# A fused attention, gMLP and expert-attention kernel: a planner with a charge for DVE and POOL in SBUF together, more operations that two engines may take, and new urgency tables

## Chip, cores and metric

The kernel runs on one core of one Trainium2 chip. The metric is the device time of one execution in microseconds (us), as the median of several runs. A core has a matrix engine (PE), three engines that work on tiles in the on-chip memory SBUF and in the matrix engine's result memory PSUM (DVE, ACT, and POOL, which only reads and writes SBUF), and a queue engine (SP) that issues all DMA transfers of this kernel.

## What is computed

Three stages follow each other for 4 batches of 576 tokens and 512 features.

```python
# 1. attention, 8 heads of 64, a window of 64 tokens
scores = q @ k.T / 8;  masked to 0 <= i - j < 64
x = softmax(scores) @ v                        # heads side by side: (4, 576, 512)
# 2. gMLP
h = relu(x @ w_in);  u, v = h[..., :512], h[..., 512:]
v_n = (v - mean(v)) / sqrt(var(v) + 1e-6)
gated = u * (w_spatial @ v_n + b_spatial)
y = gated @ w_out
# 3. four causal attention experts of width 64, the two with the largest gate logits per token
for e in range(4):
    out += gate[e] * (softmax(causal(y @ wq[e] @ (y @ wk[e]).T / 8)) @ (y @ wv[e]) @ wo[e])
```

## The kernel before

**Tiles and precision.** Every product of two full-size operands is made of three matrix passes: each operand is split in a high part and the remainder (`copy` to the high part, `sub` for the rest), and `mm3` adds high times high, high times low and low times high. So each weight and each activation costs a copy and a subtraction on ACT, DVE or POOL before PE can use it. `w_in` and `w_out` come as 64-bit floats: `prep64` loads 512 columns (512 KB), and rebuilds 32-bit values from the two words in four steps, two small ones (the scaled upper word, which only ACT makes, and the sign, which POOL or DVE makes) and two on DVE (`scalar_tensor_tensor`, profile lines L633 and L636), and then copies and subtracts. There are eight such pieces of `w_in` (four for the half V of the hidden layer, four for the half U) and four of `w_out`. `prep_sp` splits the spatial weights.

**Units.** `a_couple` does stage 1 for two groups of 192 queries: 12 score products (tile `sc`), a masked maximum on DVE (L501), the exponential on ACT (L507), two small DVE steps (L520, L522), the division of three 128 x 128 blocks `pa` (POOL or DVE, L512), their transposition on PE (L516), a copy, and 12 products with the values (tiles `pt` and `vt`, `woh`, `wol`). `b_v` projects 128 tokens onto V and normalizes them, `b_u` makes U for 288 tokens and 128 features (12 products), and `b_mix` does the spatial product (14 products of `wsp` and `vh`, `vl`) and the gate. Stage 3 is made in a second phase by `c_qk`, `c_v`, `unit`, `c_pv` and `c_wo`; `fold` first multiplies `w_out` into the weights of stage 3.

**What sets the order.** The program is not issued in the order in which it is written. Each operation is a `Node` with a dictionary of engines that may run it and their assumed costs, its dependencies and its ring buffers. `weave` walks the units and gives each node an urgency, which is the work ahead of it plus a shift from the tables `SHIFT` (one for PE nodes, one for the other engines, one for loads; 351 entries each, by unit). `Planner.run` then goes through assumed time: whenever an engine is free it takes the most urgent node that is ready and has room, unless another engine could end it sooner (`DVE_BIAS`, `POOL_BIAS`, `EFT`). The result is one fixed instruction sequence per engine. On the chip every engine runs its own sequence in order and waits where data is not there. The planner adds `DRAIN` where PE changes between three forms of products (`form` 0 for full-height ones, 1 for the scores of stage 1, 2 for products with the values), and `SWITCH` is the urgency that a change must be worth.

**Heaters.** `heat` issues 68 products of the identity with itself (8 at the start, 60 in slots in which the planner has nothing for PE). Their result is used by nobody.

Loads go over one SP queue in the planned order. A piece of `w_in` stands in one of six `y` tiles (or a `w2` tile), which its predecessor must have left.

Of the kernel before, what the change touches and what calls it, by code (L numbers as in the profile page):

```python
# [58 lines left out]


class Slot:
    def __init__(self, ring):
        self.nth, ring.asked = ring.asked, ring.asked + 1
        self.ring, self.make, self.left, self.free_at, self.t = ring, ring.make, 0, None, None

    def __getitem__(self, key):
        return self.t[key]


class Node:  # L70
    __slots__ = ("on", "emit", "prio", "wait", "next", "ready", "alloc", "use", "end", "by", "late", "form", "nth")


class Planner:
# [2 lines left out]
    ISSUE, WAY, RATE, FLIGHT = 475.0, 650.0, 360.0, 8  # L80
# [1284 lines left out]
```

## Time and profile before

| what | value |
|---|---|
| time, median of 3 runs (lowest, highest) | 463.44 us (463.25, 463.47) |
| profiled execution: time, span of its instructions | 462.36 us, 460.6 us |
| PE busy, share of the span, matrix instructions | 444.6 us, 97%, 3962 |
| DVE busy | 296.2 us, 64% |
| ACT busy | 289.1 us, 63% |
| POOL busy | 159.7 us, 35% |
| mean granted clock of PE | 0.999 of 2.4 GHz |

The span runs from the first to the last instruction of the profiled execution; its time has some 1.8 us around the span. A busy share is the union of an engine's instructions over the span. Matrix instructions overlap each other, so that a busy PE may still stand still between two results; how long PE needs for a block of products is read from the distance of the starts.

### The profile page before, as it was taken

How to read it: one execution, taken by the hardware profiler on the slowest of the kernel's cores; microseconds unless marked ns; L12 is line 12 of the kernel's file. 1: busy time of each engine (PE TensorE's matmuls, PEld its weight loads, DVE VectorE, ACT ScalarE, POOL GpSimd, SP SyncE). 2: the span in 40 equal slices, each digit the busy share in tenths (PEclk: the TensorE clock that was granted, in tenths of full speed). 3: DMA queues.
4: the chain of work that ended last, by engine and by line, in shares of the span. 5: the costliest groups of instructions: out<-in, count | busy, mean ns of one | idle time of the engine just before them, and what ended most of it. 6: DMA issues, size and time to landing. Idle time of an engine off the chain costs nothing.

```text
span 460.6 us, 10987 instructions
## 1 busy us (share of the span) xinstructions
PE 444.6 (97%) x3962; PEld 396.5 (86%) x3962; DVE 296.2 (64%) x1227; ACT 289.1 (63%) x906; POOL 159.7 (35%) x246
## 2 busy tenths in 40 slices
PE   7988998999999999999999999999999999999996
PEld 6766878997799988999899999888988988998875
DVE  3999899556583459912205346987876778858930
ACT  3867894647583337612224436898887797877953
POOL 6689587333831037700541442231031111200100
PEclk9999999999999999999999999999999999999999
DMA  8995334224242131301101000000001001000124
GB/s 268 356 308 161 124 93 156 71 78 135 65 133 61 47 91 52 89 1 54 39 1 21 26 1 2 0 2 1 1 25 46 24 2 22 25 2 1 55 85 137
DMA packets 31624, 32.97 MB, mean 72 GB/s; under 512 B 1937, under 2 KB 25489, under 8 KB 31570
## 3 DMA queue, kind: packets, MB, share of 16 engines
q1 hardware_dynamic: 31570, 32.28, 22.4%
q8 instruction: 31, 0.51, 0.4%
q14 instruction: 23, 0.19, 0.1%
HBM read 27.55 MB, written 4.72 MB: 70 GB/s over the span
## 4 chain that ended last, share of the span: by engine, by line
PE 79%; DVE 7%; DMA 4%; ACT 4%; POOL 3%; issue 1%; SPq 1%; POOLq 0%; ACTq 0%
PE mm L295 56%; PE sc L295 8%; PE at L295 8%; PE at L1180 4%; DMA y<-in_w_in_dram 3%; PE at L516 3%; ACT kd L306 1%; DVE pa L512 1%; POOL pa L512 1%; ACT p L1160 1%; SPq L384 1%; DVE wsp_l L319 1%; DVE xl L319 1%; ACT pg L306 1%; DMA qa<-in_qT_dram 1%
## 5 line engine op out<-in xcount | busy, mean ns | idle before, releaser
L295 PE MATMUL mm<-xh,w 128*128 128x288 f32 x512 | 110.3, 299 | 0.0
L295 PEld LDWEIGHTS mm<-xh,w 128*128 128x128 f32 x512 | 84.3, 188 | 1.2 <-issue 0.9
L295 PE MATMUL mm<-xl,w 128*128 128x288 f32 x256 | 75.4, 294 | 0.0
L295 PE MATMUL mm<-w,xh 128*128 128x512 f32 (+1 forms) x256 | 64.7, 342 | 0.0
L507 ACT ACTIVATE pa<-pa,mx 128x128 f32<-128x128 f32 x144 | 56.0, 395 | 9.7 <-DVE mx L501 9.5
L512 POOL TENSOR_SCALAR pa<-pa,mx 128x128 f32<-128x128 f32 x78 | 34.4, 456 | 54.5 <-ACT pa L507 29.6
L1164 POOL TENSOR_SCALAR p<-p,mc,fx 128x256 f32<-128x256 f32 (+4 forms) x24 | 16.0, 667 | 102.9 <-DVE mc L1163 48.4
L295 PEld LDWEIGHTS mm<-xl,w 128*128 128x128 f32 x256 | 48.2, 188 | 0.2
L295 PEld LDWEIGHTS mm<-w,xh 128*128 128x128 f32 x256 | 43.3, 189 | 5.0 <-issue 0.2
L1160 ACT ACTIVATE p<-p,mc 128x128 f32<-128x128 f32 (+4 forms) x72 | 41.9, 583 | 8.7 <-DVE mc L1148 4.4
L295 PE MATMUL mm<-w,xl 128*128 128x512 f32 (+1 forms) x128 | 43.2, 338 | 0.0
L295 PE MATMUL mm<-wsp_h,vh 128*128 128x288 f32 x128 | 39.0, 305 | 1.6 <-ACT ut L314 1.6
L295 PE MATMUL mm<-wsp_h,vl 128*128 128x288 f32 x128 | 37.7, 295 | 0.0
L295 PE MATMUL mm<-wsp_l,vh 128*128 128x288 f32 x128 | 37.7, 294 | 0.0
L1148 DVE CUSTOM_DVE_ANT_0 p<-sc,cmask 128x128 f32<-128x128 f32 (+4 forms) x72 | 33.7, 482 | 4.8 <-PE sc L295 3.1
L306 ACT ACTIVATE pg<-at 128x512 f32<-128x512 f32 (+4 forms) x80 | 32.3, 432 | 3.9 <-PE at L1180 3.2
L295 PE MATMUL sc<-kd,qs 128*64 128x288 f32 (+5 forms) x96 | 31.5, 342 | 0.1
L1180 PE MATMUL at<-ident,p 128*128 128x128 f32 x192 | 30.3, 276 | 1.0 <-DVE p L1164 0.3
L775 DVE TENSOR_TENSOR y<-mm,ut 128x288 f32<-128x288 f32 x24 | 10.8, 455 | 30.5 <-PE mm L295 30.5
L706 DVE BATCH_NORM_STATS2 st<-vr 128x6 f32<-128x512 f32 (+1 forms) x20 | 13.8, 690 | 25.8 <-ACT vr L314 25.4
L306 ACT ACTIVATE pt<-at 128x384 f32<-128x384 f32 x47 | 21.2, 490 | 14.0 <-PE at L516 14.0
L516 PE MATMUL at<-ident,pa 128*128 128x128 f32 x144 | 24.5, 285 | 5.7 <-DVE pa L512 3.3
(192 smaller groups left out, 1116.2 us busy)
## 6 DMA issues: line engine op xcount, KB each, us to landing
vt<-in_v_dram SPq DMA_DIRECT2D x12, 512.0 KB, 4.2
qa<-in_qT_dram SPq DMA_DIRECT2D x44, 96.0 KB, 3.2
out_dram<-ot SPq DMA_DIRECT2D x15, 256.0 KB, 2.0
y<-in_w_in_dram SPq DMA_DIRECT2D x7, 512.0 KB, 7.0
kt<-in_kT_dram SPq DMA_DIRECT2D x12, 288.0 KB, 3.1
y<-in_w_outT_dram SPq DMA_DIRECT2D x4, 512.0 KB, 3.4
y<-in_wspT_dram SPq DMA_DIRECT2D x2, 576.0 KB, 4.9
ut<-in_kT_dram SPq DMA_DIRECT2D x2, 384.0 KB, 7.5
```

The costliest lines, as they stand in the source:

```text
L295: pe.matmul(o, lhsT, rhs, start=start, stop=stop)
L306: act.activation(o, i, AF.Copy)
L319: engs[e].tensor_tensor(out=o, in0=a, in1=hi.bitcast(F32), op=ALU.subtract)
L507: act.activation(pa[:, j, :], pa[:, j, :], AF.Exp, bias=mx[:, j, 0:1], scale=-1.0, accum_out=mx[:, j, 1:2])
L512: engs[e].tensor_scalar(pa[:, j, :], pa[:, j, :], mx[:, j, 2:3], 1.0, op0=ALU.mult, op1=ALU.mult)
L516: pe.transpose(ps2[:, j * 128:(j + 1) * 128], pa[:, j, :], ident)
L706: a = N((DVE, 600), lambda e: dve.bn_stats(st[:m, 0:6], vr[:m]), [a], alloc=[st], use=[vr])
L775: dve.tensor_tensor(out=o, in0=ps[:, :HS], in1=u[:, d, tk], op=ALU.mult)
L1148: dve.tensor_tensor_reduce(out=P[:, a0:a1], in0=ps[:, :w], in1=msk, scale=-0.125, scalar=3.0e38, op0=ALU.add, op1=ALU.min, accum_out=mc[:, ...
L1160: a = N((ACT, 284 + 0.87 * L), lambda e: act.activation(P[:m, :L], P[:m, :L], AF.Exp, bias=mc[:m, 0:1], scale=-1.0, accum_out=mc[:m, 2:3]) ...
L1164: a = N({POOL: 328 + 0.832 * L, DVE: 90 + 0.52 * L}, lambda e: engs[e].tensor_scalar(P[:, :L], P[:, :L], mc[:, 3:4], fx[:, I, ev:ev + 1], ...
L1180: pe.transpose(ps[:, j * m:(j + 1) * m], P[:, j * 128:(j + 1) * 128], ident)
```

## The change

The planner gets three new rules: the 351 x 3 urgency shifts and the scalar constants are new, some nodes get other assumed costs, and some may go to more engines. What is computed is the same.

- A node that has all its operands in SBUF is marked `sbuf=True`. If such a node starts on DVE while POOL is busy (or on POOL while the last node on DVE was of that kind), the planner lengthens it by 0.55 of the overlap (`CLASH`).
- A load that is issued while earlier ones are still on their way is assumed to land 2.2 us later (`BEHIND`).
- `DRAIN` no longer charges a change into form 0, but takes 78 ns off where a form 1 or 2 node follows one of its kind, and the costs of some PE nodes move by -74 to +88 ns.
- The scaled upper word in `prep64` (function `down`) may be made by ACT, POOL or DVE. The copies of results of the value products (`a_couple`, `c_pv`) and of `fold` may go to ACT or DVE; they were ACT's alone.

The core of the diff (the three `SHIFT` tables are replaced as a whole; their rows are left out, and the marks `sbuf=True` stand on 27 more lines of the kind shown):

```diff
-SWITCH = 58767.74293990493
+SWITCH = -10949.0
 A_BIAS = 10098.0
 C_BIAS = 162315.0
-DVE_BIAS = (1730.5970176011094, 7352.217706873879)
-POOL_BIAS = (288.01246154132895, 9897.664225472437)
+DVE_BIAS = (1703.0, 1703.0)
+POOL_BIAS = (1628.0, 342.0)
...
-EFT = (772.5181606546909, 4334.303370577451)
+EFT = (810.0, 1075.0)
...
-    DRAIN = (0.0, 92.0, 91.0), (160.0, 0.0, 160.0), (75.0, 92.0, 0.0)
+    DRAIN = (0.0, 91.0, 91.0), (0.0, -78.0, 0.0), (0.0, 0.0, -78.0)
+
+    CLASH, BEHIND = 0.55, 2200.0
...
+        elif e == DVE:
+            if n.sbuf:
+                self.free[e] = n.end = n.end + self.CLASH * max(0.0, min(n.on[e], self.free[POOL] - t))
+            self.sbuf = n.sbuf
+        elif e == POOL and self.sbuf:
+            self.free[e] = n.end = n.end + self.CLASH * max(0.0, min(n.on[e], self.free[DVE] - t))
         if e == SP:
             k = round(n.on[e] / self.ISSUE)
             for _ in range(k):
                 t = max(t, self.moved[-self.FLIGHT] + self.LAT[SP]) + self.ISSUE
+                behind = self.BEHIND if self.moved[-1] > t + self.WAY else 0.0
                 self.moved.append(max(self.moved[-1], t + self.WAY) + n.late / k / self.RATE)
-            self.free[e], n.end = t, self.moved[-1]
+            self.free[e], n.end = t, self.moved[-1] + behind
...
-        S_N[n0] = S_N[n0 + 1] = top = N((PE, 890), s_mm, kn + [Q_N[n0], Q_N[n0 + 1], S_N.get(n0 - 1)], alloc=bank, use=hk, prio=prio,
+        S_N[n0] = S_N[n0 + 1] = top = N((PE, 816), s_mm, kn + [Q_N[n0], Q_N[n0 + 1], S_N.get(n0 - 1)], alloc=bank, use=hk, prio=prio,
...
-            a = N({POOL: 1053, DVE: 450}, s_norm, [a], use=[pa, mx], prio=prio)
+            a = N({POOL: 1053, DVE: 450}, s_norm, [a], use=[pa, mx], prio=prio, sbuf=True)
...
-        n1 = N((ACT, 520), lambda e: act.activation(a_(), word(1).bitcast(F32), AF.Copy, scale=2.0 ** -112),
-               [n0], alloc=[tmp], use=[raw], prio=prio)
-        n2 = N({POOL: 588, DVE: 335}, sign, [n0, n1], use=[raw, tmp], prio=prio)
+        def down(e):
+            if e == ACT:
+                act.activation(a_(), word(1).bitcast(F32), AF.Copy, scale=2.0 ** -112)
+            else:
+                engs[e].tensor_scalar(a_(), word(1).bitcast(F32), 2.0 ** -112, 1.0, op0=ALU.mult, op1=ALU.mult)
+
+        n1 = N({ACT: 540, POOL: 620, DVE: 345}, down, [n0], alloc=[tmp], use=[raw], prio=prio, sbuf=True)
+        n2 = N({POOL: 588, DVE: 335}, sign, [n0, n1], use=[raw, tmp], prio=prio, sbuf=True)
...
-        a = N((ACT, t_act(256)), lambda e: copy(e, oh[:, cs], ps[:, :256]), [o], use=[ps, oh], prio=prio)
+        a = N(on_copy(256), lambda e: copy(e, oh[:, cs], ps[:, :256]), [o], use=[ps, oh], prio=prio)
```

What this does to the fixed sequences is shown at three places near the start of the program. All line numbers move by 10 to 15 in the changed file.

**SP, the first loads.** `qa` holds queries, `ut` the keys of batch 0, `woh` and `wol` its values, and `y` and `w` pieces of `w_in` (128x1024 words are 512 KB). Before:

```order
L384 DMA qa<-in_qT_dram 128x384 x2
L384 DMA y_128<-in_w_in_dram 128x1024
L384 DMA y_130<-in_w_in_dram 128x1024
L384 DMA ut<-in_kT_dram 128x2x192 x2
L384 DMA ut<-in_kT_dram 128x4x192
L384 DMA y_135<-in_w_in_dram 128x1024
L384 DMA qa<-in_qT_dram 128x192 x2
L384 DMA w_142<-in_w_in_dram 128x1024
```

The same place of the change:

```order
L394 DMA ut<-in_kT_dram 128x2x192 x2
L394 DMA qa<-in_qT_dram 128x384 x2
L394 DMA woh<-in_v_dram 128x2x256
L394 DMA wol<-in_v_dram 128x2x256
L394 DMA w_132<-in_w_in_dram 128x1024
L394 DMA y_134<-in_w_in_dram 128x1024
L394 DMA y_136<-in_w_in_dram 128x1024
L394 DMA y_138<-in_w_in_dram 128x1024
```

Two pieces of `w_in` (1 MB) stood ahead of the first keys; now keys, queries and the first values (1.25 MB) stand ahead of the first piece.

**DVE, its first work on loaded data**, after eight rows that make masks. Rows with `sc` are masked maxima of stage 1, rows with `y` or `w` rebuild a piece of `w_in`. Before:

```order
L633 SCALAR_TENSOR_TENSOR y_140<-y_128,y_140 128x512
L636 SCALAR_TENSOR_TENSOR y_140<-y_140 128x512
L633 SCALAR_TENSOR_TENSOR y_153<-y_130,y_153 128x512
L501 ISA pa,mx<-sc,mask_74 128x128
L501 ISA mx 128x1
L501 ISA pa,mx<-sc,mask_79 128x128
```

The same place of the change, from the fourth of the first six maxima on:

```order
L511 ISA pa,mx<-sc,mask_74 128x128
L511 ISA mx 128x1
L511 ISA pa,mx<-sc,mask_79 128x128
L511 ISA mx 128x1
L511 ISA pa,mx<-sc,mask_79 128x128
L511 ISA mx 128x1
L530 TENSOR_SCALAR mx<-mx 128x3
L644 TENSOR_SCALAR w_207<-w_132 128x512
L532 RECIPROCAL mx<-mx 128x3
L638 TENSOR_SCALAR w_207<-w_132 128x512
```

DVE no longer begins with `w_in`; it does six maxima first, and then itself makes the scaled upper word (L644) and the sign (L638) of the first piece to be rebuilt there.

**PE, the step to the first U products** (`mm<-xh,w` and `mm<-xl,w`; `mm<-w,xh` and `mm<-w,xl` are V products of 128 tokens, `mm<-w,xt` those of the last 64). Before:

```order
L295 MATMUL sc<-kt,qa 64x128 x12
L295 MATMUL at<-pt,vt 64x64 x12
L295 MATMUL mm<-w,xt 128x512
L295 MATMUL mm<-w,xt 64x512
L295 MATMUL mm<-w,xt 128x512
L295 MATMUL mm<-w,xt 64x512
L295 MATMUL mm<-w,xt 128x512
L295 MATMUL mm<-w,xt 64x512 x2
L295 MATMUL mm<-w,xt 128x512
L516 MATMUL at<-ident,pa 128x128 x6
L295 MATMUL mm<-xh,w 128x288
L295 MATMUL mm<-xl,w 128x288
```

The same place of the change:

```order
L305 MATMUL sc<-kt,qa 64x128 x12
L526 MATMUL at<-ident,pa 128x128 x3
L305 MATMUL at<-pt,woh 64x64 x12
L305 MATMUL at<-pt,wol 64x64 x12
L305 MATMUL sc<-kt,qa 64x128 x12
L305 MATMUL mm<-xh,w 128x288
L305 MATMUL mm<-xl,w 128x288
L305 MATMUL mm<-xh,w 128x288 x2
L305 MATMUL mm<-xl,w 128x288
L305 MATMUL mm<-xh,w 128x288 x2
L305 MATMUL mm<-xl,w 128x288
L305 MATMUL mm<-xh,w 128x288 x2
```

The first U products stood behind all five V blocks of batch 0; now they stand behind three of them, and all eight U blocks of batch 0 stand ahead of the first spatial product, where five did.

## Rows read from the trace of the kernel before

**Rows 1.** Busy time by stretch: us, then PE, PEld, DVE, ACT, POOL, clock, DMA:

```profile
10.00:78.00 68.00, 60.81 (x726) 49.95 (x721) 64.25 (x265) 51.06 (x187) 51.80 (x71) 1.00 0.66 210
78.00:280.00 202.00, 201.34 (x1912) 186.29 (x1913) 100.27 (x422) 94.77 (x323) 75.85 (x120) 1.00 0.19 55
280.00:448.00 168.00, 166.96 (x1248) 146.83 (x1246) 127.43 (x528) 136.25 (x387) 25.92 (x32) 1.00 0.06 20
```

**Rows 2.** Timeline of PE: start, length, what, count, idle time before and releaser:

```profile
9.81 0.89 PE L295 MATMUL sc<-ut,qa 64*64 64x128 f32 x24 [1.84 <-DMA ut<-in_kT_dram]
...
65.65 0.38 PE L295 MATMUL mm<-xh,w 128*128 128x288 f32 x1
...
78.15 0.40 PE L295 MATMUL mm<-wsp_h,vh 128*128 128x288 f32 x1 [1.55 <-ACT ut L314]
```

**Rows 3.** The chain that ended last, in order of time: start, length, what:

```profile
52.99 2.01 PE mm L295 x18
...
85.96 0.82 PE sc L295 x24
86.77 2.05 PE mm L295 x14
...
99.45 0.85 PE at L295 x24
...
103.00 1.85 PE mm L295 x14
...
127.98 1.59 PE mm L295 x12
```

**Rows 4.** Groups on DVE from 10 to 78 us: count, busy us, mean ns, idle before:

```profile
L501 DVE CUSTOM_DVE_ANT_0 pa<-sc,mask 128x128 f32<-128x128 f32 x54 | 12.6, 281 | 0.2 <-PE sc L295 0.2
L512 DVE TENSOR_SCALAR pa<-pa,mx 128x128 f32<-128x128 f32 x30 | 10.5, 408 | 0.1
L633 DVE SCALAR_TENSOR_TENSOR y<-y,y 128x512 int32<-128x512 int32 x9 | 7.4, 835 | 1.6 <-POOL y L626 1.6
...
L319 DVE TENSOR_TENSOR wsp_l<-y,wsp_h 128x576 fp32r<-128x576 f32 x2 | 3.9, 1968 | 0.0
...
L628 DVE TENSOR_SCALAR y<-y 128x512 int32<-128x512 int32 x1 | 0.4, 398 | 0.0
```

**Rows 5.** The same operations over the whole span: least, median and greatest ns, first and last start:

```profile
L512 POOL TENSOR_SCALAR pa<-pa,mx x78: 359/372/1324, 19.5 to 190.7; 128x128 f32<-128x128 f32 x78
L512 DVE TENSOR_SCALAR pa<-pa,mx x66: 250/283/1326, 13.2 to 194.1; 128x128 f32<-128x128 f32 x66
...
L633 DVE SCALAR_TENSOR_TENSOR y<-y,y x11: 654/693/1259, 7.7 to 81.3; 128x512 int32<-128x512 int32 x11
...
L319 POOL TENSOR_TENSOR wsp_l<-y,wsp_h x2: 1408/1418/1428, 37.0 to 42.2; 128x576 fp32r<-128x576 f32 x2
L319 DVE TENSOR_TENSOR wsp_l<-y,wsp_h x2: 1853/1968/2083, 37.1 to 42.2; 128x576 fp32r<-128x576 f32 x2
...
L319 DVE TENSOR_TENSOR xl<-y,xh x5: 744/1028/1510, 277.1 to 337.8; 128x576 fp32r<-128x576 f32 x5
```

**Rows 6.** DMA issues of the page: count, KB each, median us to landing:

```profile
y<-in_w_in_dram SPq DMA_DIRECT2D x7, 512.0 KB, 7.0
...
ut<-in_kT_dram SPq DMA_DIRECT2D x2, 192.0 KB, 7.1
```

**Rows 7.** Timeline of DVE, its first work on loaded data:

```profile
7.66 0.69 DVE L633 SCALAR_TENSOR_TENSOR y<-y,y 128x512 int32<-128x512 int32 x1 [4.69 <-POOL y L626]
```

**Rows 8.** Groups on POOL from 10 to 78 us:

```profile
L512 POOL TENSOR_SCALAR pa<-pa,mx 128x128 f32<-128x128 f32 x30 | 16.5, 564 | 6.5 <-DVE mx L501 3.4 <-ACT pa L507 1.3 <-ACT y L630 1.2
...
L308 POOL TENSOR_SCALAR w<-y 128x512 fp32r<-128x512 f32 x6 | 4.2, 698 | 5.6 <-DVE mx L522 3.4 <-DVE y L636 1.3 <-DVE st L707 0.9
```

**Rows 9.** Groups after 280 us, the divisions of stage 3 on POOL and on DVE:

```profile
L1164 POOL TENSOR_SCALAR p<-p,mc,fx 128x256 f32<-128x256 f32 (+4 forms) x24 | 16.0, 667 | 102.9 <-DVE mc L1163 48.4 <-DVE mc L1162 17.1 <-ACT ot L306 9.7
...
L1164 DVE TENSOR_SCALAR p<-p,mc,fx 128x128 f32<-128x128 f32 x14 | 5.1, 365 | 0.4
```

More of the change, by code (lines that the diff above doesn't have):

```diff
@@ L70 @@
 class Node:
-    __slots__ = ("on", "emit", "prio", "wait", "next", "ready", "alloc", "use", "end", "by", "late", "form", "nth")
+    __slots__ = ("on", "emit", "prio", "wait", "next", "ready", "alloc", "use", "end", "by", "late", "form", "nth", "sbuf")
 class Planner:
@@ L87, in __init__, with node @@
         self.phase = self.form = self.asked = 0
-    def node(self, on, emit, deps=(), alloc=(), use=(), prio=None, late=None, form=0):
+        self.sbuf = False
+    def node(self, on, emit, deps=(), alloc=(), use=(), prio=None, late=None, form=0, sbuf=False):
         n = Node()
-        n.form, n.nth = form, self.asked
+        n.form, n.nth, n.sbuf = form, self.asked, sbuf
         self.asked += 1
@@ L545, in a_couple @@
         prio -= X_BIAS
-        o = N((PE, 760), pv, done + [PV_N.get(k[:2]) for k in grp] + vn, alloc=[ps3] + new, use=pts + hv, prio=prio,
+        o = N((PE, 848), pv, done + [PV_N.get(k[:2]) for k in grp] + vn, alloc=[ps3] + new, use=pts + hv, prio=prio,
               form=2)
@@ L651, in prep_sp @@
             n1 = N(on_copy(S, 1, False), lambda e, x=x, k=k: copy(e, wsp_h[:, k, :], raw[:, x, :]), [n0],
-                   use=[raw], prio=prio)
+                   use=[raw], prio=prio, sbuf=True)
             n2 = N({POOL: 1360, DVE: 670}, lambda e, x=x, k=k: sub(
-                e, wsp_l[:, k, :], raw[:, x, :], wsp_h[:, k, :]), [n1], use=[raw], prio=prio)
+                e, wsp_l[:, k, :], raw[:, x, :], wsp_h[:, k, :]), [n1], use=[raw], prio=prio, sbuf=True)
             P_N["wsp"].append(n2)
@@ L703, in b_v @@
             a = N((DVE, t_tt(512)), lambda e: dve.tensor_tensor(out=vr[:64], in0=ps[:64], in1=vr[:64], op=ALU.add), [a], use=[ps, vr])
-            a = N({ACT: 520, DVE: 335}, lambda e: relu(e, vr[:64], vr[:64]), [a], use=[vr])
+            a = N({ACT: 520, DVE: 335}, lambda e: relu(e, vr[:64], vr[:64]), [a], use=[vr], sbuf=True)
         a = N((DVE, 600), lambda e: dve.bn_stats(st[:m, 0:6], vr[:m]), [a], alloc=[st], use=[vr])
@@ L716, in b_v @@
             VN[b, t] = vh, vl
-            a = N(on_copy(512, 1, False), lambda e: copy(e, vh.t, vr.t), [a], alloc=[vh], use=[vr])
-            a = N({POOL: 1225, DVE: 602}, lambda e: sub(e, vl.t, vr.t, vh.t), [a], alloc=[vl], use=[vr, vh])
+            a = N(on_copy(512, 1, False), lambda e: copy(e, vh.t, vr.t), [a], alloc=[vh], use=[vr], sbuf=True)
+            a = N({POOL: 1225, DVE: 602}, lambda e: sub(e, vl.t, vr.t, vh.t), [a], alloc=[vl], use=[vr, vh], sbuf=True)
         else:
@@ L724, in hi @@
                 copy(e, t2v[0:64], vr[:64])
-            a = N(on_copy(512, 2, False), hi, [a] + old, use=[vr])
-            a = N({DVE: 602}, lambda e: sub(e, t1v[64:128], vr[:64], t1v[0:64]), [a], use=[vr])
+            a = N(on_copy(512, 2, False), hi, [a] + old, use=[vr], sbuf=True)
+            a = N({DVE: 602}, lambda e: sub(e, t1v[64:128], vr[:64], t1v[0:64]), [a], use=[vr], sbuf=True)
         TAIL.setdefault(b, []).append(a)
@@ L787, in b_mix @@
             a = N(on_copy(HS, 1, False), lambda e: copy(e, yh[:, tk], gv(g)), [a] + ([] if new else YN[b, d]),
-                  alloc=new, use=[g] + ([] if new else [yh]))
+                  alloc=new, use=[g] + ([] if new else [yh]), sbuf=True)
             a = N({POOL: t_pool(HS), DVE: t_tt(HS)}, lambda e: sub(e, yl[:, tk], gv(g), yh[:, tk]), [a],
-                  use=[g, yh, yl])
+                  use=[g, yh, yl], sbuf=True)
         YN.setdefault((b, d), []).append(a)
@@ L842, in fold @@
         FOLD.setdefault(nm, [a])
-        a = N((ACT, t_act(n)), lambda e: copy(e, view(oh.t)[:, i, :], ps[:, :n]), [a], use=[ps, oh, ol])
+        a = N(on_copy(n), lambda e: copy(e, view(oh.t)[:, i, :], ps[:, :n]), [a], use=[ps, oh, ol])
         a = N((DVE, t_tt(n)), lambda e: sub(e, view(ol.t)[:, i, :], ps[:, :n], view(oh.t)[:, i, :]), [a], use=[ps, oh, ol])
@@ L920, in go @@
                 engs[e].memset(ap, 0.0)
-        Z_N[key] = [N({POOL: c * len(aps), DVE: c * len(aps)}, go)]
+        Z_N[key] = [N({POOL: c * len(aps), DVE: c * len(aps)}, go, sbuf=True)]
     def zeros(pr):
@@ L952, in c_split @@
         h, l = YS[b, c] = r_xh.new(), r_xl.new()
-        a = N(on_copy(S, 1, False), lambda e: copy(e, h.t, y[:, c % 2, :]), YN[PH[b], c], alloc=[h], use=[y])
-        a = N({POOL: t_pool(S), DVE: t_tt(S)}, lambda e: sub(e, l.t, y[:, c % 2, :], h.t), [a], alloc=[l], use=[y, h])
+        a = N(on_copy(S, 1, False), lambda e: copy(e, h.t, y[:, c % 2, :]), YN[PH[b], c], alloc=[h], use=[y], sbuf=True)
+        a = N({POOL: t_pool(S), DVE: t_tt(S)}, lambda e: sub(e, l.t, y[:, c % 2, :], h.t), [a], alloc=[l], use=[y, h], sbuf=True)
         ZN[b, c] = [a]
@@ L1165, in unit @@
             P[:, :L], P[:, :L], mc[:, 3:4], fx[:, I, ev:ev + 1], op0=ALU.mult, op1=ALU.mult), [a, fn],
-              use=[P, mc, fx], prio=prio)
+              use=[P, mc, fx], prio=prio, sbuf=True)
         grp = 0 if I < 2 else 1
@@ L1187, in unit @@
         f, an = a, PG_N[key][:1]
-        a = N((PE, nj * 109), tr, [f] + an, alloc=[ps] + ([pg] if first else []), use=[P], prio=prio)
+        a = N((PE, nj * 109 - 40), tr, [f] + an, alloc=[ps] + ([pg] if first else []), use=[P], prio=prio)
         if first:
```

38 lines of the change are left out of this document (19 added, 19 removed), and 6 rows, old and new, of the table SHIFT.

## Prediction

> **What bounds the kernel now.** I first read the busy time by stretch. From 78 to 280 us PE is busy for 201.3 of 202 us and from 280 to 448 us for 167.0 of 168: 0.7 and 1.0 us idle [rows 1]. Nothing that another engine does there can give back more than these 1.7 us, apart from changes of form (below). From 10 to 78 us PE looks busy too, 60.8 of 68 us, and 7.2 idle [rows 1], but much of it is not work. The 68 heaters are 136 matrix instructions, and 18 of them take 2.01 us in the chain [rows 3], so all take 15.2 us. The engine that has no room in this stretch is DVE: 64.25 of 68 us busy, against 51.1 on ACT and 51.8 on POOL [rows 1].
>
> What the start costs PE can be counted in blocks. The first spatial product starts at 78.15 us, after PE sat 1.55 us for ACT's U tile [rows 2]. Ahead of it the sequence of before has five U blocks, and the chain shows the length of each: 12 products in 1.59 us for U, 24 records in 0.82 us for a score block and 24 in 0.85 us for a value block [rows 3]. So what ends the start is when the data for that first spatial product is there, and what it costs is the PE work that could not be done in the meantime.
>
> **The change part by part.** PE gets the same products, so its own work is the same; three terms move the start, two smaller ones the rest.
>
> *First work on DVE.* Before, DVE's first loaded data is a piece of w_in at 7.66 us after 4.69 us of idling [rows 7], and the first scores start only at 9.81, released by the keys' DMA [rows 2], since those (7.1 us to landing) share the engines with 1 MB of w_in [rows 6]. Now keys and queries go first, so DVE can do six maxima while w_in is on its way: 6 x 0.23 us (12.6 us over 54) [rows 4] is 1.4 us of work in what was idle time. Its next row, the scaled upper word of w_132, waits for a load issued seventh. If that takes the 7.0 us of the other pieces [rows 6] from an issue near 4 us, it comes at 11 us, and the term is a loss of about 1 us; at best all 4.69 us go. I take -1.4, nearer to the loss, since the bytes ahead of w_in are now 1.25 MB.
>
> *DVE and POOL on SBUF.* The same division of a block takes 408 ns on DVE in the start [rows 4], but 250 at least [rows 5]: 30 x 0.158 = 4.7 us. The nine L633 steps take 835 against 654: 1.6 us. The two wsp_l subtractions take 1968 [rows 4], and 744 is the least for a subtraction of that size [rows 5]: 2.4 us. So 8.7 us of DVE's 64 are stretch beside POOL, the bound on this side; the other bound is 0. Counted from the two sequences up to the first spatial gate, 12 of the 30 divisions leave DVE, 40% of 4.7 = 1.9 us. POOL gets nine divisions more, 9 x 0.564 = 5.1, but loses twelve copies and two rebuilding steps, 14 x 0.698 = 9.8 [rows 8], and a subtraction (1.4 us, as the nearest row's [rows 5]): 6 of 52 us less, 12% of the remaining 6.8 us, 0.8. The planner now also moves overlaps apart, which no row can price; I take a quarter of the remaining 6.0, 1.6. Together -4.3.
>
> *DVE's own work up to that gate.* Twelve divisions less at 0.25 [rows 5]: -3.0. Three more maxima groups, nine rows of 0.23: +2.1. Eight more one-input steps (four copies to a high part, a scaled word, three signs) at 0.398 [rows 4]: +3.2. One subtraction more and two fewer at 0.654 [rows 5], and small steps: -0.4. Together +1.9. DVE has 3.75 us of slack in the stretch [rows 1], so this counts nearly in full.
>
> The first spatial product then starts at 78.15 - 1.4 - 4.3 + 1.9 = 74.35 us, 3.8 earlier.
>
> *Work pulled ahead of it.* Eight U blocks instead of five, twelve score blocks instead of ten, eight value blocks instead of nine stand ahead of it; V blocks and transpositions are as many. 3 x 1.59 + 2 x 0.82 - 0.85 = 5.6 us of PE work [rows 3] that before came after 78 us, where PE is full. It is covered if DVE delivers its inputs, which is why the first U block, at 65.65 before [rows 2], has to come far earlier. Bounds 0 and 5.6; I take all of it, since PE had 15.2 us of heaters and 7.2 us of idling to put it in. So the start gives 9.4 us.
>
> *Changes of form.* The sequences have 98 changes between products of the three kinds before and 103 now. A spatial block takes 2.05 us after a score block and 1.85 in another place [rows 3]; 5 x 0.2 = 1.0 us is lost.
>
> *Stage 3.* 31 of 72 divisions go to POOL instead of 24, at 667 ns there against 365 for the smallest on DVE [rows 9]; 7 x 0.3 = 2.1 us if each is on PE's path, 0 if PE has other work. PE idles 1.0 us there now, so I take 0.5. The result copies that may go to DVE count 0: five in all change from ACT to DVE, where DVE has room after 78 us (100 of 202 us busy [rows 1]); without that cover they would cost some 0.5 us each, 2.5.
>
> Sum: -9.4 + 1.0 + 0.5 = -7.9 us. The profiled execution took 462.36, its span 460.6 and 1.76 around it; that is 1.08 below the median of 463.44, to which the difference is applied: 455.5 us.
>
> **A page weighed against the rows.** Both engines have a wsp_l subtraction starting at 37.0 and 37.1 us; POOL's lasts 1428 at most and DVE's 1853 at least [rows 5]. If DVE stood for all of POOL's, its own 744 would begin at 38.4 and end after some 2.0 us; with the planner's 0.55 of the overlap it would last 0.744 + 0.55 x 0.744 = 1.15. The row is near the first. The Trainium skill, SBUF — State Buffer, section "Who interferes with whom", says so too: the shared pair of ports is an exclusive lock, and the second to start stands until the first ends. By it the new charge is too small, and plans that accept an overlap at 0.55 are wrong about when DVE is free; this is the rival below.
>
> **The rivals.**
> 1. *The stretch stays.* DVE stands for whole POOL instructions, as the wsp_l rows do, and the charge of 0.55 avoids little. Then only the 1.9 us of moved divisions fall, the start gives 9.4 - 2.4 = 7.0, and where DVE falls behind the plan the U blocks, which PE meets in fixed order, stop it: another half of the 5.6 lost. Gain 4.2 - 1.5 = 2.7, so 460.7 us. For it: the wsp_l rows. Against it: POOL's lighter load.
> 2. *The second half of w_in comes late* (slower). U weights must be rebuilt some 20 us earlier than before, their loads wait for y tiles, and DVE's sequence has four L633 rows that stand until they land. Each landing takes 7.0 us [rows 6]. A stop of 2.5 us on each of the four is 10 us and decides: -7.9 + 10 = +2.1, so 465.5. Against it: DVE has maxima to do in between, and the eight pieces' 4.2 MB are what 210 GB/s [rows 1] bring in 20 us.
> 3. *No change that counts*: the planner's new assumptions miss as much as the old ones, and 5 changes of form and stage 3 eat a start of 1.5 us: 463.4.
> 4. *More than I take*: all 8.7 us of stretch and the 4.69 us of idling go, 455.5 - 4.4 - 3.3 = 447.8.
>
> **How the numbers follow.** My forecast (452 to 459) gets 0.50, rival 1 (459 to 462.5) 0.22, rival 2 0.10, rival 3 0.07, rival 4 (under 452) 0.11. 0.2% of the time, 0.9 us, is about what a measurement can tell. Faster: 0.50 + 0.22 + 0.11 = 0.83; same 0.07; slower 0.10. The range leaves out rival 2 and the far half of rival 4: 450 to 462; the forecast's own is 452 to 459.
>
> **What would show it.** In the changed profile: first scores before 6.5 us; the mean of DVE's divisions up to the first spatial product below 408 ns and those of wsp_l below 1968; the first U block before 55 us and the first spatial product at 72 to 77 us with eight U blocks ahead; PE idle under 2.5 us between there and the last 12 us. I would be wrong if PE sat for U weights, if DVE idled for w_in landings for over 5 us after 11 us, or if stage 3 showed over 3 us of PE idle. A drop of the granted clock from 1.00 [rows 1] once the heaters are used up, which before were spread to 55 us, would also break the sum.

## The result, and the profile after

The changed kernel takes 466.59 us (median of four runs, 465.98 to 467.53) beside 463.35 us for the kernel before on the same chip (462.36 to 463.47): ratio 1.0076, 95% interval 1.0055 to 1.0098. It is slower by 0.8%, outside the range of the prediction. The profiled execution took 465.98 us, 3.6 more than that of before.

The two programs do the same PE work, so they can be cut at a landmark: the last matrix instruction of the folds, which starts at 274.73 us before and at 270.46 after. What stands ahead of it is stages 1 and 2 (the *first part*), what stands behind it is stage 3. Busy time of each engine in the two parts and up to PE's last product (us, then PE, PEld, DVE, ACT, POOL with counts, clock, DMA share, GB/s), first of the kernel before:

```profile
0.00:274.73 274.73, 263.47 (x2632) 237.40 (x2632) 164.09 (x687) 143.84 (x494) 130.62 (x209) 1.00 0.33 102
274.73:456.86 182.13, 181.09 (x1333) 159.10 (x1331) 132.09 (x540) 144.72 (x411) 29.08 (x38) 1.00 0.07 24
```

The same of the changed kernel:

```profile
0.00:270.46 270.46, 261.73 (x2632) 237.48 (x2632) 179.86 (x729) 150.27 (x507) 102.79 (x168) 0.99 0.34 104
270.46:460.06 189.60, 183.35 (x1333) 159.96 (x1331) 131.45 (x532) 136.98 (x384) 36.25 (x59) 1.00 0.07 23
```

The first part is 4.27 us shorter, stage 3 is 7.47 us longer, and the output behind PE's last product takes 0.4 us more: together the 3.6. In stage 3 PE's idle time grew from 182.13 - 181.09 = 1.04 us to 6.25, and its busy time by 2.26 for the same products.

The stretches of [rows 1], after, and two more that the start needs:

```profile
10.00:78.00 68.00, 62.87 (x748) 53.84 (x748) 60.22 (x247) 54.03 (x192) 52.06 (x74) 0.97 0.67 214
78.00:280.00 202.00, 198.11 (x1882) 183.09 (x1871) 119.85 (x473) 97.45 (x319) 50.29 (x85) 1.00 0.19 56
280.00:448.00 168.00, 164.12 (x1203) 143.92 (x1202) 125.05 (x509) 126.67 (x356) 30.99 (x44) 1.00 0.06 20
...
78.00:100.00 22.00, 20.20 (x230) 18.43 (x219) 18.66 (x77) 13.06 (x49) 5.45 (x8) 1.00 0.29 85
100.00:260.00 160.00, 160.00 (x1515) 146.96 (x1513) 91.33 (x374) 77.02 (x252) 33.04 (x52) 1.00 0.20 59
```

The timeline of PE after, for [rows 2]: first scores, first U block, a wait that was not there before, the first spatial product, the longest wait behind it, and the longest at the border of stage 3 (start, length, what, count, idle time before and releaser):

```profile
7.05 0.78 PE L305 MATMUL sc<-ut,qa 64*64 64x128 f32 x20
...
48.71 0.40 PE L305 MATMUL mm<-xh,w 128*128 128x288 f32 x1
...
65.78 0.40 PE L305 MATMUL sc<-kt,qa 64*64 64x128 f32 x2 [2.31 <-issue]
66.42 1.19 PE L305 MATMUL sc<-kt,qa 64*64 64x128 f32 x22 [0.23 <-issue]
...
78.28 0.40 PE L305 MATMUL mm<-wsp_h,vh 128*128 128x288 f32 x1
...
89.40 1.51 PE L526 MATMUL at<-ident,pa 128*128 128x128 f32 x9 [1.27 <-DVE pa L522]
...
273.19 1.35 PE L305 MATMUL mm<-w,zt 128*128 128x260 f32 x9 [2.09 <-POOL zt L318]
```

The first U block comes 16.9 us earlier than before, and yet the first spatial product at 78.28 against 78.15 [rows 2]. The block at 66.42 takes 1.19 us for 22 records where a block of 24 took 0.89 before [rows 2]: the granted clock was at its lower level for 3.4 us there, which is the 0.97 of the first stretch; before it was 1.00 in all three stretches [rows 1].

The groups of [rows 4] on DVE from 10 to 78 us, after (the division of a block is L522 now, the steps of the rebuilding L648 and L651), and POOL's divisions of [rows 8]:

```profile
L651 DVE SCALAR_TENSOR_TENSOR y<-y 128x512 int32<-128x512 int32 x9 | 8.4, 937 | 0.0
L648 DVE SCALAR_TENSOR_TENSOR y<-y,y 128x512 int32<-128x512 int32 x9 | 6.2, 686 | 1.7 <-POOL y L636 1.7
...
L522 DVE TENSOR_SCALAR pa<-pa,mx 128x128 f32<-128x128 f32 x9 | 3.7, 471 | 0.0
...
L727 DVE TENSOR_SCALAR vr<-vr,st 128x512 f32<-128x512 f32 x1 | 1.6, 1648 | 0.0
L329 DVE TENSOR_TENSOR wsp_l<-y,wsp_h 128x576 fp32r<-128x576 f32 x2 | 1.6, 790 | 0.0
```

```profile
L522 POOL TENSOR_SCALAR pa<-pa,mx 128x128 f32<-128x128 f32 x45 | 24.5, 563 | 9.7 <-DVE mx L532 4.5 <-DVE mx L530 2.0 <-DVE mx L511 1.5
```

The second step of the rebuilding and the scaling of the V blocks (`vr`) in the same stretch before:

```profile
L636 DVE SCALAR_TENSOR_TENSOR y<-y 128x512 int32<-128x512 int32 x9 | 7.0, 783 | 0.0
L712 DVE TENSOR_SCALAR vr<-vr,st 128x512 f32<-128x512 f32 x1 | 1.4, 1389 | 0.0
```

The two wsp_l subtractions fell from 1968 ns to 790 and the step after the sign from 835 to 686. But the second step of the rebuilding rose from 783 ns on average to 937, and the scaling from 1389 to 1648.

### The profile page after: what moved, and what is told of

The parts are those of the page before. It is cut to its first block, busy times and chain, and to the rows that moved or that the text cites. A ratio compares the mean times of both kernels' runs of the same rounds, so it can differ in the third digit from the quotient of the medians.

```text
span 464.2 us, 10948 instructions
## 1 busy us (share of the span) xinstructions
PE 445.1 (96%) x3962; PEld 397.4 (86%) x3962; DVE 311.3 (67%) x1261; ACT 287.6 (62%) x892; POOL 139.0 (30%) x226
## 4 chain that ended last, share of the span: by engine, by line
PE 72%; DVE 13%; ACT 5%; POOL 4%; issue 3%; DMA 2%; SPq 1%; POOLq 0%; DVEq 0%; ACTq 0%
PE mm L305 50%; PE at L305 8%; PE sc L305 7%; PE at L1195 4%; PE at L526 3%; DVE p L1163 2%; POOL pa L522 2%; DMA y<-in_w_in_dram 2%; ACT p L1175 1%; DVE y L651 1%; DVE p L1179 1%; DVE pa L522 1%; DVE pa L511 1%; DVE qs L329 1%; ACT kd L316 1%
## 5 line engine op out<-in xcount | busy, mean ns | idle before, releaser
L1179 POOL TENSOR_SCALAR p<-p,mc,fx 128x128 f32<-128x128 f32 (+4 forms) x31 | 19.0, 614 | 120.5 <-DVE mc L1178 27.9
L522 POOL TENSOR_SCALAR pa<-pa,mx 128x128 f32<-128x128 f32 x69 | 34.1, 512 | 54.6 <-PE sc L305 16.6
L1175 ACT ACTIVATE p<-p,mc 128x256 f32<-128x256 f32 (+4 forms) x72 | 41.8, 582 | 12.5 <-DVE mc L1163 7.8
L1163 DVE CUSTOM_DVE_ANT_0 p<-sc,cmask 128x256 f32<-128x256 f32 (+4 forms) x72 | 34.1, 482 | 8.2 <-PE sc L305 6.0
L1195 PE MATMUL at<-ident,p 128*128 128x128 f32 x192 | 31.7, 279 | 3.0 <-POOL p L1179 1.2
L511 DVE CUSTOM_DVE_ANT_0 pa<-sc,mask 128x128 f32<-128x128 f32 x120 | 28.2, 283 | 7.1 <-PE sc L305 4.8
L305 PE MATMUL sc<-kd,qs 128*128 128x128 f32 (+5 forms) x96 | 32.0, 343 | 0.7 <-DVE mc L1163 0.7
L725 POOL TENSOR_TENSOR st<-st,nhalf 128x1 f32<-128x1 f32 (+1 forms) x20 | 11.2, 559 | 69.2 <-DVE st L724 69.2
L1195 PEld LDWEIGHTS at<-ident,p 128*128 128x128 f32 x192 | 22.1, 140 | 8.6 <-POOL p L1179 2.6
```

Of the source, the lines that this page charges most:

```text
L305: pe.matmul(o, lhsT, rhs, start=start, stop=stop)
L511: dve.tensor_tensor_reduce(out=pa[:, j, :], in0=ps[:, j * 128:(j + 1) * 128], in1=mask(j), scale=-0.125, scalar=3.0e38, op0=ALU.add, op1=A ...
L522: engs[e].tensor_scalar(pa[:, j, :], pa[:, j, :], mx[:, j, 2:3], 1.0, op0=ALU.mult, op1=ALU.mult)
L725: a = N((POOL, 464), lambda e: pool.tensor_tensor(out=st[:m, 9:10], in0=st[:m, 8:9], in1=nhalf[:m], op=ALU.pow), [n1], use=[st])
L1163: dve.tensor_tensor_reduce(out=P[:, a0:a1], in0=ps[:, :w], in1=msk, scale=-0.125, scalar=3.0e38, op0=ALU.add, op1=ALU.min, accum_out=mc[:, ...
L1175: a = N((ACT, 284 + 0.87 * L), lambda e: act.activation(P[:m, :L], P[:m, :L], AF.Exp, bias=mc[:m, 0:1], scale=-1.0, accum_out=mc[:m, 2:3]) ...
```

## The experiments

**The two halves apart.** The planner runs twice, once for the first part and once for stage 3. In most of the kernels below its choice is replaced by fixed lists of (node, engine), taken from the plan of the kernel before or after. With both lists from one kernel the program is that kernel's.

```diff
     def run(self):
-        ready = [[] for _ in range(5)]
...
+        todo = {n.nth: n for n in self.nodes}
+        self.nodes = []
+        for code in map(int, self.ORDER[self.phase].split()):
+            self.start(todo[code // 5], code % 5, 0.0, lambda n: None)
         self.phase += 1
```

New first part, old stage 3 (e1):

> Stages 1 and 2 and the folds in the order and on the engines of the changed kernel, stage 3 in those of the kernel before, taken as fixed lists. Theory (stage 3 of the new plan loses what its first part gains): PE's excess over its own work is 4.4 us smaller by 260 us in the changed kernel, and stage 3 is free of its extra 7.3 us here, so 463.4 - 4.4 = 459.0 us (457.5 to 460.5). Rival A (the loss belongs to the start, by the late query load and the clock drop after it, and stage 3 only passes it on): as the changed kernel or little under it, 465 to 467. Rival B (an order of stage 3 fits only the engine states that its own first part leaves): slower than both, over 467.

Measured: 458.18 us, ratio to before 0.9883 (0.9865 to 0.9901). Its two parts:

```profile
0.00:270.52 270.52, 261.02 (x2631) 237.51 (x2632) 178.65 (x729) 150.47 (x507) 95.90 (x157) 0.99 0.34 104
270.52:452.66 182.14, 181.11 (x1333) 159.24 (x1331) 132.06 (x540) 144.83 (x411) 27.80 (x34) 1.00 0.07 24
```

The first part takes what it takes in the changed kernel, 270.5 us, and stage 3 what it took before, to 0.01 us. So the theory held and the loss is stage 3's own; this kernel is 1.2% under the kernel before and 1.8% under the changed one.

Old first part, new stage 3 (e2):

> The other half: stages 1 and 2 and the folds as before, stage 3 in the order and on the engines of the changed kernel. Theory: 463.4 + 7.5 = 470.9 us (469 to 472.5). Rival A (the loss belongs to the start): about 463.4 (462.5 to 464.5). Rival B (fit to the own first part only): over 472.

Measured: 479.81 us, ratio 1.0353 (1.0333 to 1.0372). The direction is the theory's, but the time is 9 us beyond it, in the range of rival B: stage 3 takes 197.88 us (275.30 to 473.18). The new order starts stage 3 with the product that reads zt, whose copies are POOL's. In the changed kernel POOL's first copy to zt starts at 266.59 us, 3.9 ahead of the landmark; behind the old first part it starts at 278.30, 3.0 after it. PE's waits from 270 to 300 us (total, times, longest):

```profile
PE mm L305 <- POOL zt L318: 7.9, 2, 5.0
```

In all PE idles 11.97 us in this stage 3 instead of 6.25, and it is busy 2.56 us longer, with the granted clock at its lower level for 10.2 us from 278.2 on. So the new stage 3 loses more behind a first part that is not its own, as rival B had it; the old one does not (e1).

**The wait at 63.5 us.** SyncE's queue had two pieces of w_outT ahead of two queries and keys, which were issued at 63.1 to 64.5 us. First I held these loads for the cause (e3, and e4 on the e1 kernel).

```diff
-166/SP  145/SP  509/SP  510/SP  481/SP
+509/SP  510/SP  481/SP  166/SP  145/SP
```

(166 and 145 load w_outT, 509 and 510 queries, 481 keys.)

> The changed kernel with one move in SyncE's queue: the two queries and the keys that PE waits for at 63.5 us are issued ahead of two pieces of w_outT that stand there until DVE has freed their y tiles. All else in the same order. If the 2.31 us of idle PE and the 1.7 us of half clock behind it are on the path: 466.6 - 4.0 = 462.6 us (461.5 to 464), with no PE idle over 0.5 us from 63 to 66 and no granted clock under 1.00 from 60 to 80. Rival (DVE sets the start anyway; PE waits as long a little later, before the first spatial gates): 465.6 to 467, with the idle time found again from 66 to 90.

> The first kernel of this call (new first part, old stage 3) with the queries and keys moved ahead as in the third. If both theories hold their gains add: 459.0 - 4.0 = 455.0 us (453.5 to 457). If the wait comes back later: 459 (457.5 to 460.5). If stage 3 was not what cost the time: 462 to 466.

Measured: 465.92 us (ratio 1.0049, 1.0033 to 1.0066) and 459.13 us (0.9904, 0.9882 to 0.9925), about what the kernels without the move take, and each in the range that was given for a wait that stays or comes back. In e3 the loads go out 2.2 us earlier, and the score block still starts at 65.81 us after 2.24 us of idling. The theory fell. By the timeline, what ends the wait stands on DVE: the block needs its two score banks, and DVE reads the last scores out of them with six maxima (L511) only at 64.98 us. The timeline of DVE in the changed kernel, its first work on loaded data for [rows 7] and this place:

```profile
7.99 0.29 DVE L511 CUSTOM_DVE_ANT_0 pa<-sc,mask 128x128 f32<-128x128 f32 x1 [4.83 <-PE sc L305]
...
10.61 0.43 DVE L644 TENSOR_SCALAR w<-w 128x512 f32<-128x512 f32 x1 [0.82 <-DMA w<-in_w_in_dram]
...
60.71 0.69 DVE L648 SCALAR_TENSOR_TENSOR y<-y,y 128x512 int32<-128x512 int32 x1 [1.67 <-POOL y L636]
61.32 1.65 DVE L727 TENSOR_SCALAR vr<-vr,st 128x512 f32<-128x512 f32 x1
...
64.98 0.27 DVE L511 CUSTOM_DVE_ANT_0 pa<-sc,mask 128x128 f32<-128x128 f32 x1
```

and POOL beside it:

```profile
57.61 2.37 POOL L522 TENSOR_SCALAR pa<-pa,mx 128x128 f32<-128x128 f32 x3 [1.16 <-DVE st L724]
59.95 0.72 POOL L636 TENSOR_SCALAR y<-y 128x512 f32<-128x512 f32 x1
...
61.16 1.52 POOL L329 TENSOR_TENSOR wsp_l<-y,wsp_h 128x576 fp32r<-128x576 f32 x1
```

DVE idles 1.67 us for POOL's sign step, which stands behind three divisions, and then its scaling lasts 1.65 us beside POOL's subtraction. So the maxima were put ahead (e8, on the e1 kernel; 430 and 437 are the maxima, three each):

```diff
-155/DVE  380/DVE  156/DVE  144/DVE  385/DVE  430/DVE  437/DVE
+430/DVE  437/DVE  155/DVE  380/DVE  156/DVE  144/DVE  385/DVE
```

> The first kernel of the last call (new first part, old stage 3: 458.2 us), with one move on DVE: the six maxima that free the two score banks go ahead of five steps (two of a weight's rebuilding, a LayerNorm scaling, the bias row's low part, an addition). Theory, now that earlier queries changed nothing: PE's 2.3 us of idling at 63.5 us wait for these maxima, which DVE reaches 9 us later than planned; then the idling goes, and with it the half clock behind (1.7 us): 458.2 - 4.0 = 454.2 us (453 to 456). Rival (DVE's total sets the first spatial gates, so the wait returns before 95 us): 457 to 458.5.

Measured: 457.48 us, ratio 0.9874 (0.9856 to 0.9893), which can't be told from e1's and lies in the range of the rival. The score block now starts without a wait, at 64.26 us, so the maxima were what it waited for. But the wait returns, in the timeline of PE:

```profile
71.05 0.91 PE L305 MATMUL at<-pt,vt 128*64 128x64 f32 x22 [2.54 <-ACT pt L316]
```

The scaling, moved, takes 0.53 us instead of 1.65 (POOL's next step begins in the same moment there, at 64.01, and not ahead of it), and its neighbours are now the long ones (0.68 and 0.76 in their old place):

```profile
64.01 0.53 DVE L727 TENSOR_SCALAR vr<-vr,st 128x512 f32<-128x512 f32 x1
64.47 1.09 DVE L651 SCALAR_TENSOR_TENSOR y<-y 128x512 int32<-128x512 int32 x1
65.57 1.07 DVE L329 TENSOR_TENSOR t2w<-y,t2w 1x576 fp32r<-1x576 f32 x1
```

**POOL in the start.** On the e1 kernel, the 15 steps of POOL's divisions ahead of the first spatial product emit nothing (e11):

```diff
+        for nth in SKIP:
+            if nth in todo:
+                todo[nth].emit = lambda e: None
```

> New first part, old stage 3 (458.2 us), with 45 divisions by the row sums (15 steps) left out that stand on POOL ahead of the first spatial gate, so POOL loses 45 x 0.56 us of work beside DVE. If POOL, by its own lateness and by what DVE stands beside it, is what makes the start late: DVE's steps up to 78 us come near their least, the waits of PE between 42 and 90 us (some 5.5 us with the half clock) go, 452.7 us (451 to 454.5), the first spatial product before 75 us. Rival (DVE's and ACT's own work and the landings set the start): 456.5 to 458.5.

Measured: 452.45 us, ratio 0.9775 (0.9760 to 0.9791). The stretch from 10 to 78 us, and the first spatial product, which comes 6.0 us earlier than in e1 (78.40):

```profile
10.00:78.00 68.00, 65.15 (x790) 57.53 (x790) 62.65 (x271) 58.01 (x209) 31.30 (x31) 1.00 0.70 223
```

```profile
72.36 0.40 PE L309 MATMUL mm<-wsp_h,vh 128*128 128x288 f32 x1
```

The theory held: POOL's work holds the start of the new plan, and some 25 us of it (45 x 0.56) are worth 6 us. 1.7 of these are the clock, which stays at 1.00 here and was at its lower level for 3.4 us in e1. Whether POOL holds the start by its own lateness or by what it stretches on DVE is not separated: with the divisions gone DVE's second step of the rebuilding falls too, from 872 ns (e1) to 700. Stage 3 took 182.11 us here too.

**Stage 3: engines or order.** In stage 3, 64 steps stand on another engine than before; 46 of them moved to POOL. Crossed with the order, on the new first part, with every other thing fixed (e5: new order, old engines; e6: old order, new engines):

> The changed kernel, with each of the 64 steps of stage 3 that stand on another engine than before put back on that engine, and the order of the changed kernel kept. Stage 3 from the last fold to PE's last product took 182.1 us before, 189.6 in the changed kernel. Theory (the engines are the cause: POOL is chosen 46 times where DVE or ACT did the step before): most of the 7.5 us comes back, 460 us (458.5 to 462). Rival (the order is the cause): 465 to 468.

> The other cross: first part of the changed kernel, stage 3 in the order of before, but each of the 64 steps on the engine that the changed kernel gives it. With before's engines it took 458.2. Theory (engines): 464 to 467. Rival (order): 458 to 460. Both wrong (only the pair fits): over 468.

Measured: e5 471.68 us (1.0175, 1.0156 to 1.0193), e6 460.31 us (0.9921, 0.9898 to 0.9944). Stage 3 of each, e5 and e6:

```profile
270.12:465.63 195.51, 185.15 (x1333) 161.67 (x1331) 131.21 (x540) 146.30 (x411) 30.33 (x39) 0.99 0.06 23
```

```profile
268.27:452.68 184.41, 181.33 (x1333) 159.19 (x1331) 129.25 (x532) 135.58 (x384) 38.31 (x65) 1.00 0.07 23
```

The theory of the engines fell; e5 lies over the range of its rival as well, e6 0.3 us over. In the old order the new engines cost 184.41 - 182.14 = 2.3 us; in the new order they save 195.51 - 189.60 = 5.9 (up to 1.7 of it is a stretch of 3.4 us at the lower clock in e5's stage 3). The new order costs 13.4 us with the old engines and 189.60 - 184.41 = 5.2 with the new ones.

The border alone (e7: 18 steps back on ACT, DVE; e9: the zt product fifth on PE, as before; 1178 is that product):

```diff
-1178/PE  1141/PE  1147/PE  1155/PE  1138/PE
+1141/PE  1147/PE  1155/PE  1138/PE  1178/PE
```

> The changed kernel, with only the 18 steps at the border of stage 3 (copies to zt and xh, their subtractions, two zero fills) back on the engines of before, mostly ACT; all else in place. PE waited 2.09 us there for POOL's copies to zt. Theory (that wait is on the path): 466.6 - 2.2 = 464.4 us (463.5 to 465.2). Rival A (ACT and DVE then end as late, or the time is lost behind): 465.8 to 467. Rival B (POOL's lateness there is also what starts the stalls up to 360 us): 461 to 463.

> The changed kernel with one move on PE at the border of stage 3: the product that reads zt, which stands first there, goes behind the four blocks that follow it (three q and k blocks and a value block; before, it stood fifth). Its copies stay on POOL. Theory (what costs the time is the place in PE's order, since 18 steps on other engines changed nothing): the 2.09 us of waiting goes, 466.6 - 2.1 = 464.5 us (463.5 to 465.3). Rival A (the copies of the logits come later by four blocks, so the gate and with it the first divisions; the loss moves to 285 to 300 us): 466 to 468. Rival B (the engines behind it run freer): under 463.

Measured: e7 466.97 us (1.0088, 1.0060 to 1.0115), so rival A: PE waits as long for ACT's copies. PE's longest wait from 270 to 460 us there:

```profile
PE mm L305 <- ACT zt L316: 2.2, 1, 2.2
```

e9 464.86 us (1.0038, 1.0023 to 1.0053), as the theory had it in sum; but in the profile stage 3 is only 0.8 us shorter (188.83), and the profiled execution took 466.24 us, the longest of its eight; its first part ended at 271.51. The wait of 2.09 us is gone, and one for the copy of the logits stands in its place, 1.27 us before the next block:

```profile
280.71 0.37 PE L305 MATMUL mm<-xh,w 128*128 128x288 f32 x1 [1.27 <-DVE lg L1079]
```

Next to the one for zt the waits of stage 3 in the changed kernel are small and have many releasers (total, times, longest):

```profile
PE mm L305 <- POOL zt L318: 2.1, 1, 2.1
PE at L1195 <- POOL p L1179: 1.2, 4, 0.4
PE at L1195 <- ACT xh L316: 0.9, 1, 0.9
PE sc L305 <- DVE mc L1163: 0.7, 2, 0.4
```

Transpositions that follow their scores too closely were the next theory (e10, on e9: 15 of them moved behind one or two more PE blocks):

> The kernel just above, and in stage 3 the 15 transpositions that have under 3.0 us of other PE work between their scores and themselves (9 in the order of before) are put behind one or two more PE blocks, to some 3.4 us. Theory (PE waits since the chain of maximum, exponential, reciprocal, division is longer than the work put over it): PE's other idle time in stage 3, 4.0 us against 1.0 before, falls to about 1.5, 462 us (460.5 to 463.5). Rival (the waits come from engines that are behind as a whole, or the blocks passed over are themselves delayed): 464 to 466.

Measured: 469.47 us (1.0134, 1.0117 to 1.0151), stage 3 at 192.78 us: 3.9 us more than in e9, and outside both ranges. The theory fell. PE now idles 7.3 us in stage 3 where e9 has 5.4, and is busy 2.1 us longer.

**Table or rules.** Stage 3 planned anew on the new first part, with the rules of one kernel and the urgency table of the other, and with the new rules and an empty table.

For f2 the second planning run gets what stood before (the costs of stage 3's nodes and their engine choices too):

```diff
-DVE_BIAS = (1703.0, 1703.0)
-POOL_BIAS = (1628.0, 342.0)
+DVE_BIAS = (1703.0, 7352.217706873879)
+POOL_BIAS = (1628.0, 9897.664225472437)
...
-            if n.sbuf:
+            if n.sbuf and self.phase == 0:
...
-            self.free[e] = n.end = n.end + self.DRAIN[self.form][n.form]
+            self.free[e] = n.end = n.end + (self.DRAIN, self.OLD)[self.phase][self.form][n.form]
```

f5 has of these only the biases (DVE_BIAS and POOL_BIAS, and the constants EFT and SWITCH) and, for the units of stage 3, the `SHIFT` entries of before; f4 has no such entries.

> New first part as it is; stage 3 planned anew with the rules, costs, biases and engine choices of before and the urgency table of the changed kernel. Its PE order differs from that of the changed kernel in 545 pairs of blocks, from that of before in 1800. Theory (the new table sets the worse order): stage 3 from the last fold to PE's last product takes 187 to 193 us, 464 to 470 us in all. Rival (the new rules and costs make it worse): 182 to 185 us, 458 to 461.

> New first part as it is; stage 3 planned with the new rules for DVE and POOL, the new costs and engine choices, and the urgency table and the biases of before (454 pairs swapped against the order of before, 1687 against the changed one, 39 steps on another engine than before). Theory (table): stage 3 takes 182 to 186 us, 458 to 462 us in all. Rival (rules and costs): 187 to 192 us, 464 to 469.

> The changed kernel with an empty urgency table for stage 3 alone (1845 pairs swapped against before, 1368 against the changed kernel). If a table is worth as much as the theory needs: stage 3 takes over 190 us, 467 to 480 us in all. Rival (the table does little, and the rules make the time): 187 to 191 us, 464 to 468.

Measured: f2 471.81 us (1.0159, 1.0121 to 1.0196), f5 471.84 us (1.0175, 1.0144 to 1.0207), f4 468.22 us (1.0094, 1.0070 to 1.0118). Stage 3 of f2, f5 and f4:

```profile
271.41:466.96 195.55, 186.39 (x1333) 159.89 (x1331) 134.71 (x542) 143.63 (x402) 21.70 (x31) 1.00 0.06 23
```

```profile
270.36:467.50 197.14, 187.01 (x1333) 160.79 (x1331) 134.34 (x539) 143.88 (x402) 26.04 (x39) 1.00 0.07 23
```

```profile
270.14:462.17 192.03, 186.94 (x1333) 160.43 (x1331) 129.16 (x531) 132.49 (x376) 44.62 (x73) 0.99 0.07 23
```

f2 and f5 lie over the ranges of theory and rival alike; f4 is in the range of "a table is worth as much". Neither the table nor the rules is the cause by itself. Measured against e1, which has the same first part and the old stage 3 (182.14 us), the new table alone costs 13.4 us (f2) and the new rules, costs and engine choices alone 15.0 (f5); together, with the new biases, they cost 7.5. With the new rules the new table gives 189.60 us, no table 192.03, the old table (with its biases) 197.14. So each table does badly under rules that it was not found with, and under the new rules the old one is worse than none; no table under the old rules was not run. (Planned anew in the same way, the old rules with the old table give PE the order of the kernel before to the last block, with 13 steps on another engine. So planning anew is at most a small part of the 13.4 and 15.0 us; this kernel was not run.) The new pair is only 2.4 us better than no table, and up to 1.7 of these are 3.4 us at the lower clock in f4's stage 3; the old pair is 9.9 better.

## Why the prediction was wrong, step by step

*Stage 3, "+0.5".* This step failed, and it alone turned the sign: it measured +7.5 us. I costed it from counts (seven more divisions on POOL, five copies), between 0 and 2.1 us, as if the rest of stage 3 stayed in place. In fact 64 steps had another engine, and the table and the rules together had reordered all of it. Counts of operations per engine say little about that: in the old order the new engines cost 2.3 us (e6), near my upper bound, while the order costs 5.2 us with these engines and 13.4 with the old ones (e5). I read the order at the start only, where I expected the effect. The rivals had no case for it: their slower one lay in the loads of w_in, and rival 3 gave stage 3 only a part of 1.5 us. The text's condition "if stage 3 showed over 3 us of PE idle" is what happened, with 6.25. What in the new order costs the time stays open: of the 7.5 us 5.2 are idle time of PE and 2.3 longer busy time, the largest wait, for zt, is 2.1, without it stage 3 is only 0.8 us shorter (e9), and moving transpositions made it longer (e10).

*The first spatial product at 74.35 us.* It came at 78.28, 0.1 later than before, though DVE's busy time fell by 4.0 us, from 64.25 [rows 1] to 60.22. The step "DVE has 3.75 us of slack in the stretch, so this counts nearly in full" failed: DVE was not the only one that set the time. POOL is as full as before (52.06 against 51.80 us), DVE now idles 7.8 us where it idled 3.75, so it waited for as long as it had saved in work, and with 25 us of POOL's work away the product comes at 72.36 (e11). DVE's longest waits from 10 to 78 us, after (total, times, longest):

```profile
DVE xl L329 <- ACT xh L316: 2.4, 3, 1.0
DVE y L648 <- POOL y L636: 1.7, 1, 1.7
DVE pa L511 <- PE sc L305: 1.5, 1, 1.5
```

*First work on DVE, "-1.4".* First scores at 7.05 us, not before 6.5; six maxima then stand ahead as described. w_132 was ready at 10.61 us, 2.95 later than the first piece before [rows 7] and close to the 11 us of the bound on the loss. In the first 20 us DVE is busy for 11.39 us where it was for 13.00: it idles 1.6 us more, and the term is a loss of about that size.

*DVE and POOL on SBUF, "-4.3".* Where the plan moved overlaps apart it worked: two wsp_l subtractions 2 x (1968 - 790) = 2.4 us, nine steps 9 x (835 - 686) = 1.3 us. But other steps were stretched more: the second step of the rebuilding lost 9 x (937 - 783) = 1.4 us, and the one scaling takes 1648 ns where it took 1389. The mean of DVE's divisions, predicted under 408 ns, is 471 (nine instead of 30). Still DVE's busy time fell by 4.0 us, more than the -4.3 + 1.9 = -2.4 of the text; what failed is the step from busy time to the start of the product. The text's lighter POOL did not come either: POOL got 15 divisions more (45 against 30 [rows 8]), not nine, which is 6 x 0.563 = 3.4 us of work that the count missed. The weighed page is borne out by the scaling: it takes 0.53 us in e8 and 1.65 beside a POOL instruction that began 0.16 us ahead and lasted 1.52. With 0.55 of the overlap charged it would be 0.53 + 0.29 = 0.82. Standing until POOL's end at 62.68 and then its own 0.53 would end it at 63.21; it ended at 62.97. The Trainium skill, SBUF — State Buffer, "Who interferes with whom" (the first to issue holds the pair, the other blocks) is the nearer of the two, 0.24 us too long here.

*Work pulled ahead, "-5.6".* Right: eight U blocks stand ahead of the first spatial product. But 1.7 us are lost again from 78 to 100 us, where PE idles 22 - 20.20 = 1.8 us and did 0.1 before, and 0.5 are gained up to 260. 5.6 - 0.1 - 1.7 + 0.5 = 4.3 is the 4.27 that the first part gained, where the start was to give 9.4.

*Clock.* The drop that the text named as a danger came: PE's idling of 2.3 us from 63.5 was followed by 3.4 us at the lower of the two levels (1.2 instead of 2.4 GHz), in which PE did half: 1.7 us. The sum had no term for it. The last heater stands at 36.1 us in the changed kernel and stood at 54.7 before. In e6, whose execution had no drop, the same first part ended at 268.27 us, 6.5 ahead of the kernel before.

*Changes of form, "+1.0".* Not measured apart. PE's busy time in stage 3 grew by 2.26 us; counted in the two traces, with transpositions as a kind of their own, its sequence there has 178 runs of one kind where it had 159. But their number does not set the busy time by itself: f2 has 166 runs, and PE is busy there for 186.39 us at a clock of 1.00. What does stays open.

*Rival 2* (U weights late) did not come: the first U block starts at 48.71 us, and PE does not idle ahead of it. That its time, 465.5 us, lies near the measured one is chance. *Rival 1* had the size of the start: 4.2 us of gain, 4.27 measured, and PE stopped by its fixed order where DVE falls behind. But it took its loss from the pulled-ahead work, which held, and 0.5 us for stage 3 as well, so that its start agrees by luck.

## What to carry to other kernels

Where a planner and a tuned table set the whole program, read the new order in every stage, not only where the change aims, and look for a landmark that cuts the program into parts with the same work: one look at 270.5 and 189.6 us told more than all counts per engine. Such parts can be taken from different plans: fixed lists with the better half of each gave 458.18 us, 1.2% under the kernel before, where the new plan as a whole was 0.8% over it. Here a table found with one set of rules was no start for another: crossed, either one cost 13 to 15 us, and under the new rules the old table was worse than an empty one. And look for what ends a wait before moving anything: moving loads that did not end it (e3), or copies to an engine that ends them as late (e7), changed nothing, and where the wait was taken away another came up some us later (e8, e9).
